# A streaming channel gate: the first 8 rows in a tile of their own, kept on chip and stored last

## Chip, cores, metric

One core of one Trainium2 chip; the rest of the chip is idle. The metric is the device time of one execution in microseconds. Every profile shows the span from the first to the last instruction, which is 1.4 to 1.5 us shorter. One row below is 768 bytes in each of the 128 partitions, 98,304 bytes.

A run is called slow when it lies over 1.5% above the fastest of its kernel; ratios are of fast runs. The experiments were measured in three calls (batches, each with the kernel before in turn), the first two on chip 10 and the third on chip 12; the record doesn't give the chip of the result. PE is the matrix engine, DVE the vector engine, ACT the scalar engine, POOL GpSimd, and SP the engine on whose queue most loads are issued; a transfer lands when the last of the 16 DMA engines has done its share of it.

## The reference, cut to what matters

```python
# x: bf16 [1, 384, 384, 384], w1d: bf16 [1]
g = einsum("bhwc->bc", x) / (H * W)      # mean over all pixels
s = sigmoid(g * w1d[0])                  # k = 1: one weight, no neighbours
return x * s[:, None, None, :]
```

The gate needs the sum over all of x, and of x (113.25 MB) the kernel keeps only a few tiles on the chip at a time. Read strictly, x would have to be read twice.

## The kernel before

It reads x once. It guesses the gate from the mean of the first 4 rows, stores every tile with this guess, sums all of x meanwhile, and compares the true gate with the guess in bf16 at the end. Only if they differ, which this data never makes them do, does it go through x again. x is 1152 rows, 18 tiles of 64 in 4 slots. Of each tile, PE sums 48 rows (matmuls with ones) and DVE 16 rows (`OWN`); DVE also multiplies by the gate. Loads are issued on the SP queue (the second half of tile 0 and all of tile 2 on ACT's), stores on ACT's.

```python
TILE, SLOTS, EARLY, LEAD, FORE, OWN = 64, 4, 4, 8, 32, 16
PAUSE = 9
...
load(0, TILE, 0, hi=LEAD)                             # 8 rows of tile 0, for the guess
plan.dma("sync", w_one[0:1, 0:1], w1d.unsqueeze(0), writes=["w_one"])
load(0, TILE, 0, ("sync", "scalar"), lo=LEAD)         # its other 56, 28 on each queue
load(slot(1), TILE, row0(1))
load(slot(2), TILE, row0(2), ("scalar", "scalar"))
load(slot(3), TILE, row0(3))
...
for k in range(n_tiles):
    if k >= SLOTS:
        for i in range(2) if k == SLOTS else () if k < SLOTS + 2 else (k - SLOTS,):
            sum_own(i)                                # DVE: 16 rows
            put(slot(i), TILE, row0(i), parts=None if i else (FORE, TILE - FORE))
        if k == SLOTS:
            pause(slot(k))       # one ACT activation of 9 rows, once store 0 has landed
        load(slot(k), TILE, row0(k), reads=["pause"] if k == SLOTS else ())
    ...                                               # PE sums the tile
...
put(slot(last), TILE, row0(last), slot(n_tiles))      # last tile: gate, store
sum_own(last)
join_own()                                            # then the check of the guess
```

Of the kernel before, what the change touches and what calls it, by code (L numbers as in the profile page):

```python
# [3 lines left out]
P = 128  # L4
# [5 lines left out]
ACT_F = mybir.ActivationFunctionType  # L10
# [139 lines left out]
def split(n, most):  # L150
    k = -(-n // most)
    return [n // k + (i < n % k) for i in range(k)]
# [3 lines left out]



TILE, SLOTS, EARLY, LEAD, FORE, OWN = 64, 4, 4, 8, 32, 16


PAUSE = 9


def bass_standalone__channel_attn_eca__vision_kernel(
# [5 lines left out]
    B, H, W, C = x.shape  # L171
    assert B == 1 and C == ROW and (B * H * W) % (4 * P) == 0
    n_rows = B * H * W // P
    x_rows, o_rows = x.flatten_outer_dims(), out.flatten_outer_dims()

    def dram(view, r0, n):
        return view[r0 * P : (r0 + n) * P, :].rearrange("(p t) c -> p (t c)", p=P)

    ones = nc.alloc_sbuf_tensor("ones", [P, P], BF16)
    s_early = nc.alloc_sbuf_tensor("s_early", [P, C], BF16)  # L180
    w_one = nc.alloc_sbuf_tensor("w_one", [1, 16], BF16)
    w_scaled = nc.alloc_sbuf_tensor("w_scaled", [P, 2], F32)
    warm = nc.alloc_sbuf_tensor("warm", [P, 2], F32)
# [3 lines left out]
    zeros = nc.alloc_sbuf_tensor("zeros", [P, 2], BF16)  # L187
    own = nc.alloc_sbuf_tensor("own", [P, C], F32)
    part = nc.alloc_sbuf_tensor("part", [P, C], F32)
    terms = nc.alloc_sbuf_tensor("terms", [P, 3 * C], BF16)  # L190
    n_arena = nc.sbuf_bytes_remaining // (2 * C)
    arena = nc.alloc_sbuf_tensor("arena", [P, n_arena * C], BF16)
    acc = [
        [nc.alloc_psum_tensor(f"acc{g}_{i}", [P, WIDE], F32) for i in range(3)]
        for g in range(2)
    ]
# [3 lines left out]
    def at(r0, n):  # L200
        assert r0 + n <= n_arena
        return arena[:, r0 * C : (r0 + n) * C]

    def rows(r0, n):
        return [("sb", r) for r in range(r0, r0 + n)]

    def gate(to, place, n, s):
        s_b = s[:].unsqueeze(1).broadcast_to([P, n, C])
        v, to_v = (at(r, n).rearrange("p (t c) -> p t c", t=n) for r in (place, to))
        return lambda e: e.tensor_tensor(to_v, v, s_b, ALU.mult)  # L210

    n_tiles = n_rows // TILE
    base = SLOTS * TILE
    assert n_rows % TILE == 0 and base + PAUSE <= n_arena
    assert EARLY % 4 == FORE % 4 == (TILE - OWN) % 4 == 0 and EARLY <= LEAD <= FORE
    last = n_tiles - 1
    ready = nc.alloc_semaphore("ready")

    def slot(k):
        return k % SLOTS * TILE  # L220

    def row0(k):
        return k * TILE


    s_true = at(slot(last), 1)
    plan = Planner(nc, "a", 70)

    def load(place, n, r0, queues=("sync",), lo=0, hi=None, reads=()):

        i, hi = lo, hi or n
        for queue, m in zip(queues, split(hi - lo, -(-(hi - lo) // len(queues)))):
            plan.dma(
                queue,
                at(place + i, m),
                dram(x_rows, r0, n)[:, i * C : (i + m) * C],
                reads=reads,
                writes=rows(place + i, m),
            )
            i += m  # L240
# [3 lines left out]
    def mm(e, bank, weights, moving, start, stop):  # L244
        if not loaded:
            loaded.append(e.matmul(bank, weights, moving, start=start, stop=stop))  # L246
            return loaded[0]
        return e.add_instruction(  # L248
            mybir.InstMatmult(
                name=nc.get_next_instruction_name(),  # L250
                engine=mybir.EngineType.PE,
                ins=[e.lower_ap(moving), e.lower_ap(weights)],
                outs=[e.lower_ap(bank)],
                start_tensor_calc=start,
                stop_tensor_calc=stop,
                ldweights=False,
            )
        )

    def add_rows(e, group, column, n, start, stop):  # L260

        n_wide = n * C // WIDE
        all_of = [
            mm(
                e,
                acc[group][i % 3][:, :],
                ones[:],
                arena[:, column + i * WIDE : column + (i + 1) * WIDE],
                start and i < 3,
                stop and i >= n_wide - 3,  # L270
            )
            for i in range(n_wide)
        ]
        return all_of[-1]

    def sum_early():
        plan.op(
            "tensor",
            lambda e: add_rows(e, 0, 0, EARLY, True, True),
            reads=["ones"] + rows(0, EARLY),  # L280
            writes=["acc0"],
        )

    def nothing(e, bank, start):

        none = zeros[:, 0:1].broadcast_to([P, WIDE])
        return mm(e, acc[1][bank][:, :], ones[:], none, start, not start)

    def sum_all():

        def one(e, s):
            e.wait_ge(ready, 1).then_inc(ready, -1)  # L292
            for r, n in ((0, FORE), (FORE, TILE - OWN - FORE)):
                add_rows(e, 1, (slot(s) + r) * C, n, False, False).then_inc(
                    plan.sems["tensor"], 1
                )

        def emit(e):
            for i in range(3):
                nothing(e, i, True)  # L300
            rounds = -(-n_tiles // SLOTS)
            some = n_tiles - (rounds - 1) * SLOTS
            with e.Fori(0, rounds) as k:
                for s in range(some):
                    one(e, s)
                if some < SLOTS:
                    with e.If(k < rounds - 1):
                        for s in range(some, SLOTS):
                            one(e, s)
            for i in range(3):  # L310
                done = nothing(e, i, False)
            done.then_inc(plan.sems["tensor"], 1)

        plan.streams["tensor"].append(("block", emit, None))
# [62 lines left out]
                writes=["acc_own"],  # L377
            )

    def put(place, n, r0, to=None, parts=None):  # L380
        to, i = place if to is None else to, 0
        for m in parts or [n]:
            plan.op(
                "vector",
                gate(to + i, place + i, m, s_early),
                reads=["s_early"] + rows(place + i, m),
                writes=rows(to + i, m),
            )
            i += m
        plan.final.append(  # L390
            plan.dma("scalar", dram(o_rows, r0, n), at(to, n), reads=rows(to, n))
        )

    def pause(r0):

        to = at(base, PAUSE)
        plan.op(
            "scalar",
            lambda e: e.activation(  # L399
                to, warm[:, 0:1].broadcast_to([P, PAUSE * C]), ACT_F.Sigmoid  # L400
            ),
            reads=["warm"],
            writes=rows(r0, 1) + ["pause"],
        )

    def weight():

# [24 lines left out]
    plan.op("gpsimd", lambda e: e.memset(warm[:, 0:1], 0.0), writes=["warm"])  # L432
    plan.op("vector", lambda e: e.memset(ones[:], 1.0), writes=["ones"])  # L433
    plan.op("gpsimd", lambda e: e.memset(zeros[:], 0.0), writes=["zeros"])
    load(0, TILE, 0, hi=LEAD)
    plan.dma("sync", w_one[0:1, 0:1], w1d.unsqueeze(0), writes=["w_one"])
    load(0, TILE, 0, ("sync", "scalar"), lo=LEAD)
    load(slot(1), TILE, row0(1))

    load(slot(2), TILE, row0(2), ("scalar", "scalar"))  # L440
    load(slot(3), TILE, row0(3))
    heads = {e: len(plan.streams[e]) for e in ("sync", "scalar")}
    weight()
    sum_early()
    add_banks(0, copy=True)
    plan.op(
# [4 lines left out]
        reads=["total", "w_scaled0", "warm1"],  # L451
        writes=["s_early"],
    )
    plan.need("tensor", ["zeros"])
    sum_all()

    for k in range(n_tiles):
        if k >= SLOTS:

            for i in range(2) if k == SLOTS else () if k < SLOTS + 2 else (k - SLOTS,):  # L460
                sum_own(i)
                put(slot(i), TILE, row0(i), parts=None if i else (FORE, TILE - FORE))
            if k == SLOTS:
                pause(slot(k))
            load(slot(k), TILE, row0(k), reads=["pause"] if k == SLOTS else ())
        there = rows(slot(k), TILE)
        plan.relay(ready, "gpsimd", "tensor", there, rows(slot(k), FORE), ["acc1"])
        plan.signals("tensor", rows(slot(k) + FORE, TILE - OWN - FORE), ["acc1"])
    plan.signals("tensor", [], ["acc1"])
    for k in range(n_tiles - SLOTS, last):  # L470
        sum_own(k)
        put(slot(k), TILE, row0(k))

    put(slot(last), TILE, row0(last), slot(n_tiles))
    sum_own(last)
    join_own()

# [5 lines left out]
        reads=["acc_own", "total"],  # L483
        writes=["total"],
# [6 lines left out]
        reads=["total", "w_scaled1"],  # L491
        writes=["s_true"] + rows(slot(last), 1),
# [6 lines left out]
        reads=["s_true", "s_early"],  # L499
        writes=["total"],  # L500
# [4 lines left out]
        reads=["total"],  # L505
        writes=["wrong"],
# [4 lines left out]
        reads=["wrong"],  # L511
        writes=["redo"],
# [6 lines left out]
    half, r0 = (base - above) // 2, 0  # L519
    for k, n in enumerate(split(n_rows, half)):  # L520
        place = above + k % 2 * half
# [4 lines left out]
            reads=rows(place, n),  # L526
            writes=rows(place, n),
# [98 lines left out]
```

## Time and profile before

| | before |
|---|---|
| time, 6 runs | 528.34 us median, 527.86 to 529.28 |
| span of the first profile | 526.5 us |
| DVE busy | 440.0 us (84%) |
| PE busy | 180.0 us (34%) |
| DMA | full from 1 to 524 us, 433 GB/s |

The prediction below shows the lines that carry this and reads them.

### The profile page before, as it was taken

What the parts mean: (1) busy time and instruction counts of PE and PEld (TensorE: products, weight loads), DVE (VectorE), ACT (ScalarE), POOL (GpSimd) and SP (SyncE); (2) the same over time, 40 slices, a digit from 0 to 9 for tenths busy, and PEclk for the clock granted to TensorE, in tenths of its full rate; (3) what the DMA queues carried; (4) which work ended last, traced back from release to release, by engine and by line L of the source; (5) the groups of instructions that cost most, each with busy time, mean ns of one, the idle gap of its engine ahead of it and who ended that gap; (6) DMA issues with size and microseconds to landing.
All of it is one profiled execution on the core that took longest, in us unless ns stands there. A gap on an engine that the chain in (4) does not pass through costs nothing.

```text
span 526.5 us, 902 instructions
## 1 busy us (share of the span) xinstructions
PE 180.0 (34%) x648; PEld 0.2 (0%) x2; DVE 440.0 (84%) x78; ACT 5.8 (1%) x5; POOL 0.3 (0%) x6
## 2 busy tenths in 40 slices
PE   2255752043240707061422506070513315070701
PEld 0000000000000000000000000000000000000000
DVE  1869999999996978969696969789696969698795
ACT  1000020000000000000000000000000000000000
POOL 0000000000000000000000000000000000000000
PEclk9996967558585858567575858576675858585765
DMA  9999999999999999999999999999999999999998
GB/s 375 433 459 405 418 448 448 418 418 467 429 418 418 467 429 418 429 459 426 418 429 459 426 418 441 445 429 418 448 437 429 418 459 429 426 418 459 429 426 359
DMA packets 5620, 226.51 MB, mean 430 GB/s; under 512 B 626, under 2 KB 626, under 8 KB 754
## 3 DMA queue, kind: packets, MB, share of 16 engines
q10 hardware_dynamic: 3024, 122.29, 53.7%
q1 hardware_dynamic: 2594, 104.20, 46.0%
q14 instruction: 2, 0.02, 0.0%
HBM read 113.25 MB, written 113.25 MB: 430 GB/s over the span
## 4 chain that ended last, share of the span: by engine, by line
DMA 42%; another core or an unknown queue 27%; DVE 21%; issue 7%; SPq 0%; ACT 0%; DVEq 0%
DMA arena<-in_x_dram 24%; DMA out_dram<-arena 18%; DVE part L338 12%; DVE arena L210 7%; DVE own L345 1%; DVE total L326 0%; SPq L109 0%; DVE own L363 0%; DVE terms L356 0%; ACT arena L488 0%; DVE total L496 0%; DVE total L482 0%; DVE wrong L504 0%; DVE total L324 0%
## 5 line engine op out<-in xcount | busy, mean ns | idle before, releaser
L248 PE MATMUL acc<-arena,ones 128*128 128x512 bf16 x637 | 176.1, 441 | 312.2 <-PEq L292 310.8
L210 DVE TENSOR_TENSOR arena<-arena,s_early 128x24576 bf16<-128x24576 bf16 (+1 forms) x19 | 233.2, 12278 | 11.5 <-PE acc L248 6.5
L338 DVE TENSOR_REDUCE part<-arena 128x384 f32<-128x6144 bf16 x17 | 179.2, 10539 | 56.9 <-DMA arena<-in_x_dram 56.9
L338 DVE TENSOR_REDUCE own<-arena 128x384 f32<-128x6144 bf16 x1 | 10.4, 10435 | 0.6 <-DMA arena<-in_x_dram 0.6
L345 DVE TENSOR_TENSOR own<-own,part 128x384 f32<-128x384 f32 x17 | 9.5, 558 | 0.6
L425 DVE TENSOR_SCALAR w_scaled<-w_all 128x1 f32<-128x1 f32 x2 | 0.2, 152 | 8.0 <-PE w_all L416 8.0
L248 PE MATMUL acc_own<-terms,ones 128*128 128x384 bf16 x3 | 1.4, 479 | 15.3 <-DVE terms L356 15.3
L488 ACT ACTIVATE arena<-total,w_scaled 128x384 bf16<-128x384 f32 x1 | 0.6, 615 | 440.3 <-DVE total L482 440.3
L326 DVE TENSOR_TENSOR total<-total,acc 128x128 f32<-128x128 f32 (+2 forms) x10 | 3.9, 393 | 0.3
L399 ACT ACTIVATE arena<-warm 128x3456 bf16<-128x3456 f32 x1 | 3.1, 3082 | 61.9 <-DMA out_dram<-arena 61.9
L416 PE MATMUL w_all<-w_one,ones 1*128 1x1 bf16 x1 | 0.2, 158 | 9.3 <-DMA w_one<-in_w1d_dram 9.3
L248 PE MATMUL acc<-zeros,ones 128*128 128x512 bf16 x6 | 2.3, 507 | 0.0
L324 DVE COPY total<-acc 128x384 f32<-128x384 f32 x2 | 1.1, 554 | 1.2 <-PE acc L248 1.2
L410 ACT ACT_TABLE_LOAD x1 | 1.3, 1283 | 2.3 <-issue 2.3
L433 DVE MEMSET ones<- 128x128 bf16 x1 | 0.2, 165 | 1.3 <-PEq L611 1.3
L363 DVE TENSOR_TENSOR own<-own,terms 128x384 f32<-128x384 f32 x2 | 1.1, 559 | 0.1
L356 DVE CAST terms<-own 128x384 bf16<-128x384 f32 x3 | 1.1, 359 | 0.1
L496 DVE TENSOR_TENSOR total<-arena,s_early 128x384 f32<-128x384 uint16 x1 | 0.6, 558 | 0.7 <-ACT arena L488 0.7
L448 ACT ACTIVATE s_early<-total,w_scaled 128x384 bf16<-128x384 f32 x1 | 0.6, 614 | 9.8 <-DVE total L326 9.8
L482 DVE TENSOR_TENSOR total<-total,acc_own 128x384 f32<-128x384 f32 x1 | 0.6, 554 | 0.1
L246 PE MATMUL acc<-arena,ones 128*128 128x512 bf16 x1 | 0.6, 608 | 0.0
L504 DVE TENSOR_REDUCE wrong<-total 128x1 f32<-128x384 f32 x1 | 0.6, 553 | 0.0
(10 smaller groups left out, 1.2 us busy)
## 6 DMA issues: line engine op xcount, KB each, us to landing
out_dram<-arena ACTq DMA_DIRECT2D x18, 6144.0 KB, 49.9
arena<-in_x_dram SPq DMA_DIRECT2D x16, 6144.0 KB, 41.8
arena<-in_x_dram ACTq DMA_DIRECT2D x2, 3072.0 KB, 41.5
arena<-in_x_dram ACTq DMA_DIRECT2D x1, 2688.0 KB, 14.0
arena<-in_x_dram SPq DMA_DIRECT2D x1, 2688.0 KB, 21.4
arena<-in_x_dram SPq DMA_DIRECT2D x1, 768.0 KB, 7.8
w_one<-in_w1d_dram SPq DMA_DIRECT2D x1, 0.0 KB
```

What stands on the lines that cost most here:

```text
L210: return lambda e: e.tensor_tensor(to_v, v, s_b, ALU.mult)
L246: loaded.append(e.matmul(bank, weights, moving, start=start, stop=stop))
L248: return e.add_instruction(mybir.InstMatmult(name=nc.get_next_instruction_name(), engine=mybir.EngineType.PE, ins=[e.lower_ap(moving), e.l ...
L324: emit = lambda e, part=part, of=of: e.tensor_copy(part, of)
L326: emit = lambda e, part=part, of=of: e.tensor_tensor(part, part, of, ALU.add)
L338: lambda e: e.reduce_sum(to[:], view, axis=mybir.AxisListType.X),
L345: lambda e: e.tensor_tensor(own[:], own[:], part[:], ALU.add),
L356: lambda e, term=term: e.tensor_copy(term, own[:]),
L363: lambda e, term=term: e.tensor_tensor(own[:], own[:], term, ALU.subtract),
L399: lambda e: e.activation(to, warm[:, 0:1].broadcast_to([P, PAUSE * C]), ACT_F.Sigmoid),
L410: lambda e: e.activation(warm[:, 1:2], warm[:, 0:1], ACT_F.Sigmoid),
L448: lambda e: e.activation(s_early[:], total[:], ACT_F.Sigmoid, scale=w_scaled[:, 0:1]),
```

## The change

The intent: the first 8 rows, from which the gate is guessed, get a place of their own above the four slots and stay there until the end. Their store is the last. Tile 0 shrinks to 56 rows, followed by 17 tiles of 64. The pause used to fill the place above the slots, which is now taken, so it fills `terms`, a small buffer that is used only in `join_own`, in three pieces of 3 rows. PE sums the 8 rows first, in place of three matmuls on zeros, and 8 zeroed pad rows let DVE sum 16 rows of tile 0 as of any other.

```diff
-TILE, SLOTS, EARLY, LEAD, FORE, OWN = 64, 4, 4, 8, 32, 16
-PAUSE = 9
+FIRST, EARLY, HEAD, TILE, SLOTS, FORE, OWN = 8, 4, 56, 64, 4, 32, 16
+PAUSE, PAUSES = 3, 3
...
-        to = at(base, PAUSE)
-        plan.op("scalar", lambda e: e.activation(to, warm[...], ACT_F.Sigmoid), ...)
+        to, of = terms[:, : PAUSE * C], warm[:, 0:1].broadcast_to([P, PAUSE * C])
+        for i in range(PAUSES):
+            plan.op("scalar", lambda e: e.activation(to, of, ACT_F.Sigmoid), ...)
...
-    load(0, TILE, 0, hi=LEAD)
+    plan.op("gpsimd", lambda e: e.memset(at(HEAD, len(pad)), 0.0), writes=pad)
+    load(base, FIRST, 0)
-    load(0, TILE, 0, ("sync", "scalar"), lo=LEAD)
+    load(slot(0), size(0), row0(0), ("sync", "scalar"))
...
-    put(slot(last), TILE, row0(last), slot(n_tiles))
+    gated(base, FIRST)
+    gated(slot(last), TILE, slot(n_tiles))
+    store(slot(n_tiles), TILE, row0(last))
+    store(base, FIRST, 0)
```

More of the change, by code (lines that the diff above doesn't have):

```diff
@@ L210, in gate @@
         return lambda e: e.tensor_tensor(to_v, v, s_b, ALU.mult)
-    n_tiles = n_rows // TILE
+    n_tiles = 1 + (n_rows - FIRST - HEAD) // TILE
     base = SLOTS * TILE
-    assert n_rows % TILE == 0 and base + PAUSE <= n_arena
-    assert EARLY % 4 == FORE % 4 == (TILE - OWN) % 4 == 0 and EARLY <= LEAD <= FORE
+    assert (n_rows - FIRST - HEAD) % TILE == 0 and base + FIRST <= n_arena
+    assert EARLY % 4 == FIRST % 4 == FORE % 4 == (TILE - OWN) % 4 == 0
+    assert EARLY < FIRST and TILE - OWN <= HEAD
     last = n_tiles - 1
@@ L222, in row0, with size, load @@
     def row0(k):
-        return k * TILE
+        return FIRST + (HEAD + (k - 1) * TILE if k else 0)
+    def size(k):
+        return TILE if k else HEAD
     s_true = at(slot(last), 1)
     plan = Planner(nc, "a", 70)
-    def load(place, n, r0, queues=("sync",), lo=0, hi=None, reads=()):
-        i, hi = lo, hi or n
-        for queue, m in zip(queues, split(hi - lo, -(-(hi - lo) // len(queues)))):
+    def load(place, n, r0, queues=("sync",), reads=()):
+        i = 0
+        for queue, m in zip(queues, split(n, -(-n // len(queues)))):
             plan.dma(
@@ L278, in sum_early, with close @@
             "tensor",
-            lambda e: add_rows(e, 0, 0, EARLY, True, True),
-            reads=["ones"] + rows(0, EARLY),
+            lambda e: add_rows(e, 0, base * C, EARLY, True, True),
+            reads=["ones"] + rows(base, EARLY),
             writes=["acc0"],
         )
-    def nothing(e, bank, start):
+    def close(e, bank):
         none = zeros[:, 0:1].broadcast_to([P, WIDE])
-        return mm(e, acc[1][bank][:, :], ones[:], none, start, not start)
+        return mm(e, acc[1][bank][:, :], ones[:], none, False, True)
     def sum_all():
@@ L298, in emit @@
         def emit(e):
-            for i in range(3):
-                nothing(e, i, True)
+            add_rows(e, 1, base * C, FIRST, True, False).then_inc(
+                plan.sems["tensor"], 1
+            )
             rounds = -(-n_tiles // SLOTS)
@@ L310, in emit @@
             for i in range(3):
-                done = nothing(e, i, False)
+                done = close(e, i)
             done.then_inc(plan.sems["tensor"], 1)
@@ L378, in join_own, with gated, store, put @@
             )
-    def put(place, n, r0, to=None, parts=None):
-        to, i = place if to is None else to, 0
-        for m in parts or [n]:
+    def gated(place, n, to=None):
+        to = place if to is None else to
+        plan.op(
+            "vector",
+            gate(to, place, n, s_early),
+            reads=["s_early"] + rows(place, n),
+            writes=rows(to, n),
+        )
+    def store(place, n, r0):
+        plan.final.append(
+            plan.dma("scalar", dram(o_rows, r0, n), at(place, n), reads=rows(place, n))
+        )
+    def put(k):
+        if k:
+            gated(slot(k), TILE)
+        else:
+            gated(slot(k), FORE)
+            gated(slot(k) + FORE, HEAD - FORE)
+        store(slot(k), size(k), row0(k))
+    def pause(r0):
+        to, of = terms[:, : PAUSE * C], warm[:, 0:1].broadcast_to([P, PAUSE * C])
+        for i in range(PAUSES):
             plan.op(
-                "vector",
-                gate(to + i, place + i, m, s_early),
-                reads=["s_early"] + rows(place + i, m),
-                writes=rows(to + i, m),
-            )
-            i += m
-        plan.final.append(
-            plan.dma("scalar", dram(o_rows, r0, n), at(to, n), reads=rows(to, n))
-        )
-    def pause(r0):
-        to = at(base, PAUSE)
-        plan.op(
-            "scalar",
-            lambda e: e.activation(
-                to, warm[:, 0:1].broadcast_to([P, PAUSE * C]), ACT_F.Sigmoid
-            ),
-            reads=["warm"],
-            writes=rows(r0, 1) + ["pause"],
-        )
+                "scalar",
+                lambda e: e.activation(to, of, ACT_F.Sigmoid),
+                reads=["warm"],
+                writes=["pause", "term0", "term1", "term2"] + ([] if i else rows(r0, 1)),
+            )
     def weight():
@@ L434, in bass_standalone__channel_attn_eca__vision_kernel @@
     plan.op("gpsimd", lambda e: e.memset(zeros[:], 0.0), writes=["zeros"])
-    load(0, TILE, 0, hi=LEAD)
+    pad = rows(HEAD, TILE - HEAD)
+    plan.op("gpsimd", lambda e: e.memset(at(HEAD, len(pad)), 0.0), writes=pad)
+    load(base, FIRST, 0)
     plan.dma("sync", w_one[0:1, 0:1], w1d.unsqueeze(0), writes=["w_one"])
-    load(0, TILE, 0, ("sync", "scalar"), lo=LEAD)
+    load(slot(0), size(0), row0(0), ("sync", "scalar"))
     load(slot(1), TILE, row0(1))
@@ L453, in bass_standalone__channel_attn_eca__vision_kernel @@
     )
-    plan.need("tensor", ["zeros"])
+    plan.need("tensor", ["zeros"] + rows(base, FIRST))
     sum_all()
+    plan.signals("tensor", rows(base, FIRST), ["acc1"])
     for k in range(n_tiles):
@@ L461, in bass_standalone__channel_attn_eca__vision_kernel @@
                 sum_own(i)
-                put(slot(i), TILE, row0(i), parts=None if i else (FORE, TILE - FORE))
+                put(i)
             if k == SLOTS:
@@ L465, in bass_standalone__channel_attn_eca__vision_kernel @@
             load(slot(k), TILE, row0(k), reads=["pause"] if k == SLOTS else ())
-        there = rows(slot(k), TILE)
+        there = rows(slot(k), TILE - (0 if k else OWN))
         plan.relay(ready, "gpsimd", "tensor", there, rows(slot(k), FORE), ["acc1"])
@@ L471, in bass_standalone__channel_attn_eca__vision_kernel @@
         sum_own(k)
-        put(slot(k), TILE, row0(k))
-    put(slot(last), TILE, row0(last), slot(n_tiles))
+        put(k)
+    gated(base, FIRST)
+    gated(slot(last), TILE, slot(n_tiles))
+    store(slot(n_tiles), TILE, row0(last))
+    store(base, FIRST, 0)
     sum_own(last)
```

## The prediction

> **What bounds the kernel now.** The kernel reads x once, multiplies each tile by a gate that it guesses from the first 4 rows, stores the product, and sums all of x on the side to check the guess at the end. (A row here is 768 bytes in each of 128 partitions, 98,304 bytes; x has 1152 of them, 18 tiles of 64.) I read the page's head first, to see which engine is full.
>
> ```profile
> span 526.5 us, 902 instructions
> PE 180.0 (34%) x648; PEld 0.2 (0%) x2; DVE 440.0 (84%) x78; ACT 5.8 (1%) x5; POOL 0.3 (0%) x6
> DMA  9999999999999999999999999999999999999998
> HBM read 113.25 MB, written 113.25 MB: 430 GB/s over the span
> ```
>
> No compute engine is full; the DMA row is, in all slices but the last. Bytes read and written are one x each (1152 x 98,304 = 113.25 MB), so there is no traffic to save. A slice of 13 us can hide a gap, so I asked for stretches next. Columns: stretch, length, busy PE, PEld, DVE, ACT, POOL, granted clock, DMA share, GB/s.
>
> ```profile
> 0.00:1.00 1.00, 0.00 (x0) 0.00 (x0) 0.00 (x0) 0.00 (x0) 0.20 (x4) 1.00 0.07 6
> 1.00:524.00 523.00, 179.96 (x648) 0.20 (x2) 440.00 (x78) 5.80 (x5) 0.13 (x2) 0.70 1.00 433
> 524.00:526.00 2.00, 0.00 (x0) 0.00 (x0) 0.00 (x0) 0.00 (x0) 0.00 (x0) 0.50 0.08 29
> ```
> ```profile
> 154.90:183.90 29.00, 10.35 (x35) 0.00 (x0) 24.03 (x4) 0.00 (x0) 0.00 (x0) 0.65 1.00 434
> 183.90:212.90 29.00, 9.51 (x35) 0.00 (x0) 23.98 (x4) 0.00 (x0) 0.00 (x0) 0.71 1.00 434
> ```
>
> The DMA share is 1.00 for 523 us at 433 GB/s, and a period of one tile (one load, one store, 12.58 MB) takes 29.0 us at 434 GB/s whatever the tile. (A packet counts where it starts, so the last 2 us look emptier than they are: packets started before 524 end up to 525.9.) The packet records of the trace say the same: each of the 16 engines runs packets of 49,152 bytes back to back, 1.815 us each, 27.1 GB/s, from 1.0 us until between 524.6 and 525.9 us. Work of another engine counts only if it leaves these engines without a queued transfer. The waits show how far the vector engine is from that:
>
> ```profile
> DVE part L338 <- DMA arena<-in_x_dram: 56.9, 13, 5.3
> DVE arena L210 <- DMA arena<-in_x_dram: 5.0, 1, 5.0
> ```
>
> DVE waits some 5 us for its load in each of the later periods, and not the reverse: it needs 24.0 of the 29.0 us. Last, the end, in the timeline (start, duration, engine, operation):
>
> ```profile
> 471.92 12.95 DVE L210 TENSOR_TENSOR arena<-arena,s_early 128x24576 bf16<-128x24576 bf16 x1
> 484.91 18.34 ACTq L109 DMA_DIRECT2D out_dram<-arena  x2
> 489.92 12.96 DVE L210 TENSOR_TENSOR arena<-arena,s_early 128x24576 bf16<-128x24576 bf16 x1 [5.04 <-DMA arena<-in_x_dram]
> 502.79 10.41 DVE L338 TENSOR_REDUCE part<-arena 128x384 f32<-128x6144 bf16 x1
> ...
> 521.28 0.15 DVE L510 CAST redo<-wrong 128x1 int32<-128x1 f32 x1
> ```
>
> The last load lands at 489.9, the last gate ends at 502.9 and its store is issued then. One 6.29 MB store takes 6.29 / 434 = 14.5 us alone, so it needs the engines from 511.3 to 525.9: when issued it stood 8.4 us behind earlier stores (the completions of the three last stores are at 496.7, 511.3 and 525.9 in the trace). So even here no engine is hungry. The check is done at 521.4, and its readers on the queues are through by about 524.1; that chain has 1.8 us to spare against the last packet. The end is set by bytes, plus 1.0 us before the first packet and 0.5 us after the last.
>
> **What the Trainium skill says.** "DMA: Bandwidth & Descriptors", section "Where 436 GB/s comes from", puts the ceiling at 16 ports x 32 B x 850 MHz = 435.2 GB/s; the trace runs at 433 to 434, within 0.5% of it. The same page, "Queues, rings and completion order", says that each DMA engine takes turns between the queues that have work for it, a packet at a time. This fits: as long as either loads (SP) or stores (ACT) are queued the rate stays at 434, and from 490 on, stores alone run as fast. "VectorE: DVE Perf Modes", section "The perf-mode tier table (the rule you actually need)", has bf16 tensor_tensor at 2x; the gate's 24,576 elements in 12.95 us are 0.527 ns each, two per 0.96 GHz cycle. "Perfetto Trace Analysis", section "Identifying Performance Opportunities", says to improve the most-contended engine; here that is DMA, and the change leaves its bytes alone.
>
> **The change, part by part.**
> 1. *Tile sizes.* 8 + 56 + 17 x 64 = 1152: the same bytes. The opening loads are as before, even in their pieces (8 rows, then 28 on each queue, then tiles 1 to 3); only the 8 rows sit beyond the four slots. They are now contiguous in HBM, but their packets stay 6,144 bytes. The first store is 56 rows, with packets of 43,008 bytes, and there is one more store of 128 packets of 6,144 bytes. At 0.233 us per such packet (median of the first load) and 1.815 x 7/8 = 1.588 for the 56-row ones, an engine's 8 packets of each kind cost 8 x (1.588 + 0.233 - 1.815) = 0.05 us more. On the path: +0.05 us.
> 2. *The gate.* The first tile is gated as 32 + 24 rows instead of 32 + 32, which saves 6.56 x 8/32 = 1.6 us of DVE around 42 us. Its store stands behind a load of tile 2 in the ACT queue, which lands at 53.4, so its issue 1.6 us sooner starts nothing sooner. The 8 rows are gated before the last tile: 3,072 x 0.527 = 1.6 us plus about 0.1. DVE idles 5.0 us there, so it is hidden. On the path: 0.
> 3. *The first store's end, and the pause.* With 8 rows less to move, store 0 lands 8 x 98,304 / 434 GB/s = 1.8 us sooner, near 74 instead of 76. The pause of 3.08 us becomes three: one activation of 3,456 elements at 3.08 and of 1 element at 0.20 give 0.834 ns an element, so 1,152 take 1.16 us, three 3.5, and about 3.6 with two semaphore steps. Load 4 is issued at about 74 + 3.6 = 77.9 instead of 79.2. All that time store 1 (issued at 68.9, 14.5 us of work) is queued. On the path: 0; the phase of loads against stores moves by 1.3 us.
> 4. *The end.* At any time after the first store, 8 more rows have been loaded for the same number stored. So the last load lands 1.3 to 1.8 us sooner, near 488.4; the last gate ends near 501.4; its store starts at about 509.5 behind the older ones, ends at 524.1, and the 8 rows take 1.8 us to 525.9. The check chain ends near 519.8. It had slack already, so this buys nothing.
> 5. *The sum.* Six matmuls on the 8 rows replace three on zeros: about 1.5 us of a PE with 310 us of waits. The GpSimd memset of 8 pad rows is one instruction in the first microseconds, with tile 0 not wanted before 20 us. On the path: 0.
>
> Sum: 527.93 + 0.05 = 528.0 us.
>
> **The rivals.**
> - *The short last store trims the tail.* If the last completion waited on a whole large store, 8 rows would end sooner than 64. For it: a 6.29 MB store is the last thing to land. Against it: each engine moves a fixed share of every store (8 of the 128 packets) and stays busy to its own end, so a smaller last piece leaves each engine's total alone. Its last packet would be 0.23 instead of 1.8 us, and if part of the 1.3 us spread among engines' ends comes from that size, up to 1 us could go: 527.0.
> - *Slack of 8 rows removes a stall.* For it: the tiles' slots are full all the time, and stores gate loads. Against it: the share is 1.00 in every stretch I asked. There is one visible loss, in 44 to 80 us, at 427 instead of 434 GB/s (around 53 us all engines ran one packet of 2.1 to 2.7 us): 36 x 7/434 = 0.6 us. If its cause is the meeting of the first store with loads, it could go or grow: 527.4 to 528.6.
> - *The pause's new phase empties a queue.* Three short activations with waits, an earlier load 4, and a completion of store and load together might leave the engines without work for the 2 us between a landing and the next issue. Against it: in-flight transfers amount to 42 us per load and 50 per store in each 29 us, about three transfers at any time. It would need both queues empty. If it happened in every one of 14 periods, 14 x 1 us: 542; I don't expect it.
> - *The check fails and the second pass runs.* The sum's parts still add to 1152 rows (8 + 48 + 8 for the first 64, with zeros in the pad), so no; it would double the time.
>
> **Range and chances.** The three runs before spread over 0.9 us, and the effects that I can't exclude are each below 1 us either way: 527.2 to 529.1. Two per cent is 10.6 us. Faster by that would need 226.5 MB in about 516 us, 439 GB/s, above anything the trace sustained: 0.01. Slower needs a repeated gap or a second pass: 0.01.
>
> **What would show it right or wrong.** Right: DMA share 1.00 and 433 GB/s from 1 to 524; the last load landing near 488.4 with a DVE gate of about 1.7 us just before it, in a wait that shrinks from 5.0; load 4 issued near 77.9; a store of 8 rows landing at 525.9, about 1.8 us after that of 64 rows; check done near 519.8. Wrong: any stretch after 1 us below 430 GB/s, the last gate waited for by the DMA engines, or engines' last packets ending before 524.5.

## The result, and the profile after

| | before | after |
|---|---|---|
| time, 6 runs | 528.34 us (527.86 to 529.28) | 528.86 us (528.25 to 530.18) |
| ratio, fast runs | | 1.0009, 95% interval 0.9993 to 1.0025: same |
| span of the first profile | 526.5 us | 527.7 us |

A ratio here is the mean time of one kernel's fast runs over that of the other's of the same rounds, so it is not quite the ratio of the medians quoted.

The head of the page of the changed kernel:

```profile
span 527.7 us, 911 instructions
PE 181.6 (34%) x651; PEld 0.2 (0%) x2; DVE 440.1 (83%) x79; ACT 6.2 (1%) x7; POOL 2.9 (1%) x7
DMA  9999999999999999999999999999999999999997
HBM read 113.25 MB, written 113.25 MB: 429 GB/s over the span
```

PE does three matmuls more, DVE one gate more, POOL one memset of 2.7 us, and the bytes are the same. The stretches (columns as in the prediction: length, busy PE, PEld, DVE, ACT, POOL, clock, DMA share, GB/s), first the whole, then two periods of one tile:

```profile
1.00:524.00 523.00, 181.60 (x651) 0.20 (x2) 440.07 (x79) 6.20 (x7) 2.73 (x3) 0.70 1.00 432
524.00:527.40 3.40, 0.00 (x0) 0.00 (x0) 0.00 (x0) 0.00 (x0) 0.00 (x0) 0.50 0.39 161
```
```profile
155.00:184.00 29.00, 10.19 (x35) 0.00 (x0) 23.84 (x4) 0.00 (x0) 0.00 (x0) 0.66 1.00 434
184.00:213.00 29.00, 9.36 (x35) 0.00 (x0) 24.03 (x4) 0.00 (x0) 0.00 (x0) 0.69 1.00 434
```

The bound is untouched: share 1.00, 29.0 us and 434 GB/s for a period. One stretch is slower than the others, before (first line) and after (second):

```profile
44.00:80.00 36.00, 25.32 (x97) 0.00 (x0) 35.55 (x7) 3.08 (x1) 0.00 (x0) 0.79 1.00 427
44.00:80.00 36.00, 25.58 (x99) 0.00 (x0) 35.93 (x6) 3.49 (x3) 0.00 (x0) 0.80 1.02 425
```

Its share is full all the same: packets that take longer count as busy, so only the GB/s show it. DVE's waits for loads are as before too, but for the last (us in total, times, longest):

```profile
DVE part L343 <- DMA arena<-in_x_dram: 58.7, 13, 5.2
...
DVE arena L210 <- DMA arena<-in_x_dram: 3.3, 1, 3.3
```

The pause and load 4, in the timeline, and then the end:

```profile
75.05 3.55 ACT L414 ACTIVATE terms<-warm 128x1152 bf16<-128x1152 f32 x3 [61.37 <-DMA out_dram<-arena]
...
78.63 0.33 SPq L109 DMA_DIRECT2D arena<-in_x_dram  x1
```
```profile
471.60 14.62 DVE L210 TENSOR_TENSOR arena<-arena,s_early 128x24576 bf16<-128x24576 bf16 x2
484.58 18.93 ACTq L109 DMA_DIRECT2D out_dram<-arena  x3
489.55 12.96 DVE L210 TENSOR_TENSOR arena<-arena,s_early 128x24576 bf16<-128x24576 bf16 x1 [3.33 <-DMA arena<-in_x_dram]
...
520.92 0.15 DVE L529 CAST redo<-wrong 128x1 int32<-128x1 f32 x1
```

The first of these lines now holds two gates, the one of tile 16 and that of the 8 rows; 14.62 - 12.95 = 1.7 us is what the new one takes, and DVE's wait for the last load shrank from 5.0 to 3.3 us by as much. The three pauses take 3.55 us.

Two things in the 16 DMA engines' packet records did not look as before. All engines lose some time near 53 us, and one of them, a straggler, ends well after the others:

| profile | loss near 53 us, us per engine | end of the first, median, second-last, last engine |
|---|---|---|
| before | 0.54 | 524.6, 524.9, 525.6, 525.9 |
| after | 1.21 | 524.9, 525.4, 526.0, 527.3 |

The loss is the sum of what load packets of 49,152 bytes took between 40 and 64 us beyond 1.83 us (usual are 1.815), over 16; an engine's end is that of its last store's completion. By these, the 1.2 us between the two profiled spans are one engine's late end (1.3 us after the second-last, against 0.3) and 0.3 to 0.5 us that all engines share.

### The profile page after: what moved, and what is told of

The parts are those of the page before. It is cut to its first block, busy times and chain, and to the rows that moved or that the text cites. A ratio compares the mean times of both kernels' runs of the same rounds, so it can differ in the third digit from the quotient of the medians.

```text
span 527.7 us, 911 instructions
## 1 busy us (share of the span) xinstructions
PE 181.6 (34%) x651; PEld 0.2 (0%) x2; DVE 440.1 (83%) x79; ACT 6.2 (1%) x7; POOL 2.9 (1%) x7
## 4 chain that ended last, share of the span: by engine, by line
DMA 74%; DVE 24%; issue 0%; ACT 0%; SPq 0%; DVEq 0%
DMA arena<-in_x_dram 41%; DMA out_dram<-arena 33%; DVE arena L210 12%; DVE part L343 10%; DVE own L350 1%; DVE total L331 0%; DVE own L368 0%; DVE terms L361 0%; ACT arena L507 0%; DVE total L515 0%; DVE total L501 0%; DVE wrong L523 0%; DVE total L329 0%; SPq L109 0%; DVE redo L529 0%
## 5 line engine op out<-in xcount | busy, mean ns | idle before, releaser
L252 PE MATMUL acc<-arena,ones 128*128 128x512 bf16 x643 | 179.0, 444 | 312.3 <-PEq L296 310.8
L210 DVE TENSOR_TENSOR arena<-arena,s_early 128x24576 bf16<-128x24576 bf16 (+3 forms) x20 | 233.3, 11672 | 9.5 <-PE acc L252 6.2
L414 ACT ACTIVATE terms<-warm 128x1152 bf16<-128x1152 f32 x3 | 3.5, 1162 | 61.4 <-DMA out_dram<-arena 61.4
L449 POOL MEMSET arena<- 128x3072 bf16 x1 | 2.7, 2657 | 0.0
L252 PE MATMUL acc<-zeros,ones 128*128 128x512 bf16 x3 | 0.8, 379 | 0.0
L250 PE MATMUL acc<-arena,ones 128*128 128x512 bf16 x1 | 0.6, 607 | 0.0
```

Source lines behind the costliest of these rows:

```text
L210: return lambda e: e.tensor_tensor(to_v, v, s_b, ALU.mult)
L250: loaded.append(e.matmul(bank, weights, moving, start=start, stop=stop))
L252: return e.add_instruction(mybir.InstMatmult(name=nc.get_next_instruction_name(), engine=mybir.EngineType.PE, ins=[e.lower_ap(moving), e.l ...
L414: lambda e: e.activation(to, of, ACT_F.Sigmoid),
L449: plan.op("gpsimd", lambda e: e.memset(at(HEAD, len(pad)), 0.0), writes=pad)
```

## The experiments

My theory: the time is the bytes at 433 to 434 GB/s, and nothing that was moved lies on that path. The rivals: the short last store changes the tail; the small store or the pause's phase costs by itself; the loss near 53 us makes the difference. Each diff below is against the changed kernel unless it says otherwise, and every ratio is to the kernel before.

### The control, twice

No edit.

> The changed kernel, unaltered, as the control on this chip. Theory (the time is the bytes at 433 to 434 GB/s, and nothing that was moved lies on that path): ratio to the kernel before 1.000 to 1.002. In its profile the loss near 53 us, where every engine's load packet took 2.8 to 3.1 us instead of 1.815 (1.1 us per engine; 0.5 us in the kernel before), should differ from the first profile if it is chance, and so should the one engine that ended 1.3 us after the rest. Rival (the 128 small packets and the late store cost 0.5 to 1 us by themselves): ratio 1.002 or more, and again one engine that ends over 1 us late.

> The changed kernel once more, as the control of this call. Theory: ratio to the kernel before 0.998 to 1.002, and the loss near 50 to 53 us again about 1.1 us per engine, as in all five profiles so far of kernels with the first tile apart.

Measured: 528.42 us median (528.22 to 529.04), ratio 0.9992 (0.9964 to 1.0020), and 528.70 us (528.20 to 530.04), ratio 1.0001 (0.9972 to 1.0030). The loss near 53 us is 1.19 and 1.25 us per engine, so it is not chance; the last engine ends 0.7 and 0.4 us after the second-last instead of 1.3, so that is.

### The kernel before, as a kernel tested

> The kernel before, as one of the kernels tested, to have a second profile of it. Theory: ratio 0.998 to 1.002 to itself. If the loss near 53 us is chance or the chip's, it is anywhere from 0.5 to 1.2 us; if the change doubled it, it is 0.5 us again while the control of this call has 1.1. One engine's end stands out by an amount that differs from profile to profile (0.3 us in its first).

Measured: 528.01 us (527.88 to 528.88), ratio to itself 0.9987 (0.9959 to 1.0016): this is how far one such ratio can be trusted. Loss 0.61 us per engine; ends 524.5, 524.9, 525.7, 526.0. So the change has doubled the loss: 0.54 and 0.61 before, 1.21, 1.19 and 1.25 after (and 1.20 to 1.36 in five more fast profiles of kernels below whose first store is the same 56 rows at the same time).

### No pause

```diff
-PAUSE, PAUSES = 3, 3
+PAUSE, PAUSES = 3, 0
```

> The three pauses taken away; load 4 is then issued as soon as store 0 has landed, at about 75.1 instead of 78.6 us. Theory: same time within 0.2% of the control, since store 1 (14.5 us of work) is queued meanwhile; DMA share 1.00 in 60 to 490 us. Rival (the pause keeps loads and stores in a good phase): 1 us or more slower, with a stretch below 430 GB/s after 75 us.

Measured: 528.89 us (528.09 to 530.25), ratio 1.0001 (0.9972 to 1.0031). In the timeline, load 4 is issued 3.7 us sooner than in the changed kernel:

```profile
74.97 0.33 SPq L109 DMA_DIRECT2D arena<-in_x_dram  x1
```

The last gate starts 2.6 us sooner too (486.92), and the end stays: the time did not come from there. A pause of this length neither costs nor gains anything that these runs resolve.

### A long pause

```diff
-PAUSE, PAUSES = 3, 3
+PAUSE, PAUSES = 3, 15
```

> Fifteen pauses instead of three, 15 x 1.18 = 17.7 us from the landing of store 0 at 75.2. Store 1 is then alone and done at 75.2 + 14.5 = 89.7; load 4 and store 2 (which stands behind the pause on ACT) are issued at 93.0 and start about 1.5 us later. Theory: the 16 engines stand still for 4 to 5 us, which nothing gives back: 533 us, 4.0 to 5.5 above the control. Rival (the vector engine's wait of 5 us in each period is slack in which the pipeline catches up): less than 1 us lost.

Measured: 541.39 us, the median of all five runs; four fast ones from 538.5 to 541.6, ratio 1.0222 (1.0200 to 1.0243), 12 us. The rival that slack makes it up is out, but the size is two to three times what I expected. The profile fell in a slow run (595.8 us), so I read it only up to the gap that the program itself makes, in these stretches:

```profile
60.00:88.00 28.00, 11.94 (x47) 0.00 (x0) 27.97 (x4) 12.78 (x11) 0.00 (x0) 0.79 0.99 429
88.00:94.00 6.00, 0.00 (x0) 0.00 (x0) 6.00 (x2) 4.65 (x4) 0.00 (x0) 0.50 0.43 131
```

Store 1 was done at 88 to 89 us, load 4 and store 2 started at 93.6, 0.8 us after their issue (I had put 1.5): the engines' idle time between 88.0 and 93.7 adds up to 86 engine-us, 5.4 us for each of 16. The other 6 to 7 us of the fast runs have no profile in a fast run, and stay open. Still, one gap of the queues was not given back here: these runs lost at least its length.

### The order of the last two stores, twice

```diff
     gated(base, FIRST)
+    store(base, FIRST, 0)
     gated(slot(last), TILE, slot(n_tiles))
     store(slot(n_tiles), TILE, row0(last))
-    store(base, FIRST, 0)
```

> The 8 rows stored before the last tile instead of after it. Theory: same within 0.2% of the control; the last packets are then 49,152 bytes and the engines' ends spread as in the kernel before (1.3 us). Rival (a short last store trims the tail): 0.5 to 1 us slower than the control.

> The 8 rows stored before the last tile, a second time: the first time its median was 1.5 us above the control's, with runs from 528.5 to 532.1 that overlap it. Theory: chance, so within 1 us of this call's control. Rival (a short last store trims the tail): again 1 us or more above the control.

Measured: 529.93 us (528.48 to 532.05), ratio 1.0027 (0.9995 to 1.0059); the second time 529.12 us (528.01 to 532.30), ratio 1.0009 (0.9975 to 1.0044). The medians are 1.5 and 0.4 us above the controls of their calls, but the lowest runs are not, or hardly (528.48 against 528.22, 528.01 against 528.20). In the profiles the engines end as in the control: first at 524.9, median at 525.4 and 525.3; the last at 526.5 in the first, without any straggler, and at 527.7 in the second, 1.4 us after the second-last. So in the profiles the size of the last store doesn't set where the engines end. The times leave it open: over both calls the twelve runs have a median of 529.37 us and the twelve of the controls 528.54, so 0.8 us, which is in the rival's range although the second pair alone is not. Whether this order makes a late engine more frequent was not tested.

### The 8 rows not stored

Its output is wrong, which doesn't matter for the time.

```diff
     store(slot(n_tiles), TILE, row0(last))
-    store(base, FIRST, 0)
```

> The store of the 8 rows left out (a wrong result, on purpose). Theory: 0.79 MB at 434 GB/s, so 1.8 us less than the control (ratio to it 0.9966), nothing else changed. Rival (another chain, such as the check, which ended 2.1 us ahead of the last packets or so, takes over, or the fixed completion time of a store hides it): less than 1 us gained. Rival (small packets at the end are dearer than their bytes): 2.5 us or more gained.

Measured: 526.89 us (526.38 to 528.73), ratio 0.9960 (0.9932 to 0.9988); over the control's 0.9992 that is 0.9968, 1.7 us, and 1.5 by the medians. Five of the six runs are below every run of both controls. Predicted were 1.8. This is the plainest sign of the bound: 0.7% of the written bytes less, and the time follows by their transfer time. The page confirms what was left out:

```profile
HBM read 113.25 MB, written 112.46 MB: 428 GB/s over the span
```

Its profile is at the same time the best sight of a straggler. 15 engines end between 523.1 and 524.6, 1.7 us before those of the control, and one at 526.9, so this execution took 527.3 us of span, no less than the control's 527.4. One look would have said that the store is free.

### The 8 rows stored first

```diff
+            if k == SLOTS:
+                gated(base, FIRST)
+                store(base, FIRST, 0)
             for i in range(2) if k == SLOTS else ...
...
-    gated(base, FIRST)
     gated(slot(last), TILE, slot(n_tiles))
     store(slot(n_tiles), TILE, row0(last))
-    store(base, FIRST, 0)
```

> The changed kernel with the 8 rows gated and stored first of all, not last: the rows lie apart, but nothing is kept back. Theory: same time within 0.2% of the control; the small store takes its 1.8 us early, so load 4 and the last load come later by about 1.8 us than in the control (last load near 491 instead of 489.4), and the check ends as late as in the kernel before or later, still ahead of the last packets. Rival (what is kept back to the end matters): 1 us or more slower than the control.

Measured: 529.38 us (528.40 to 530.69), ratio 1.0005 (0.9975 to 1.0035). Against the control of its call: 0.7 us in the median, 0.0004 in the ratio, which can't be told from zero. The profiled execution was the slowest of the six (span 529.2): 13 engines ended by 526.0, the others at 526.7, 527.0 and 528.8. (The loss, 0.88 us per engine, came at 58.5 us here, after the first three small packets that each engine moved of the first store.) A straggler does more than end late. Fifteen engines had done their share of the last load by 491.1, the sixteenth at 494.75, and in the timeline the last gate starts right then, at 494.8 instead of 489.2:

```profile
494.77 12.96 DVE L210 TENSOR_TENSOR arena<-arena,s_early 128x24576 bf16<-128x24576 bf16 x1 [4.98 <-DMA arena<-in_x_dram]
```

I had expected 491, which fifteen engines met. As I read it, it still cost only what the last engine was late, because stores were queued meanwhile.

### Tile 2 on the SP queue

```diff
-    load(slot(2), TILE, row0(2), ("scalar", "scalar"))
+    load(slot(2), TILE, row0(2), ("sync", "sync"))
```

> The changed kernel with both loads of tile 2 on the SP queue, so that store 0 stands behind no load and can start when it is issued, at about 42 instead of 51 us. Theory: same time within 0.2% of the control (the bytes are the same, all engines busy either way). If the loss of 1.1 us per engine near 52 us belongs to the meeting of the first store with the loads, it moves to 42 to 47 us; if it belongs to the ACT queue's handing over from loads to stores, it vanishes (0.2% or 1 us faster); if to that time or to tile 3's load, it stays near 50 to 55 us.

Measured: 529.40 us (527.88 to 533.81), ratio 1.0029 (0.9997 to 1.0061); this call has no control of the changed kernel. Tile 0 was ready sooner than I had reckoned, and store 0 went out at 36.3 us. The loss is not near 52 us any more (0.05 us per engine from 42 to 64 us); it is at 37 to 41 us, where load packets of 24,576 bytes took up to 2.2 us instead of 0.91, 1.2 us per engine in all, just ahead of the first store's packets. So it goes with the start of the first store beside loads, and not with tile 3, a fixed time or the ACT queue's change from loads to stores; its size is that of the changed kernel. Nothing was gained, then, and the slower median comes with stragglers: in this profile 13 engines ended at 525.8 to 525.9 and three at 527.2, 527.8 and 529.6. The late ones had made the last load late, and the last store with it, so that the others stood idle for 0.5 us near 509 (7.2 engine-us). The lowest run, 527.88, equals the lowest of the kernel before.

### DVE work beyond the period

```diff
-FIRST, EARLY, HEAD, TILE, SLOTS, FORE, OWN = 8, 4, 56, 64, 4, 32, 16
+FIRST, EARLY, HEAD, TILE, SLOTS, FORE, OWN = 8, 4, 56, 64, 4, 32, 28
```

> The vector engine sums 28 rows of each tile instead of 16: 10.44 x 28/16 = 18.3 us instead of 10.44, so 31.8 us for a tile instead of 24.0, more than the 29.0 that a load and a store take. Theory (DMA binds because DVE has 5.0 us to spare in a period, and no more): DVE becomes the bound; 18 x 7.9 = 142 us more DVE work, of which the 62 us of its waits for loads swallow part: 528.6 + 80 = 608 us, 600 to 614, and no more waits of DVE for loads after the first tiles. Rival (DVE's share of 83% is not real work on the way, and DMA stays the bound): 535 or less.

Measured: 593.90 us (593.79 to 594.17), ratio 1.1244. DVE does become the bound, as these groups and this stretch show (groups: busy us, mean ns, then DVE's idle time before them):

```profile
L343 DVE TENSOR_REDUCE part<-arena 128x384 f32<-128x10752 bf16 x17 | 309.3, 18194 | 0.1
```
```profile
187.00:303.00 116.00, 32.85 (x106) 0.00 (x0) 115.86 (x13) 0.00 (x0) 0.00 (x0) 0.60 0.97 398
```

DVE is busy 115.86 of 116 us, and the 59 us of waits for loads are 0.1. My 608 us was too high. DVE's work grew by 137 us, to 576.8, not by 142. Its idle time up to the check's end fell by 68 us (from 81 in the control to 13), not by 62, since waits for PE went as well; and the check is now what ends last, 2.4 us before the end of the span instead of 6.6. 137 - 68 - 4 = 65 is what was measured (593.9 - 528.6). So DVE's 5 us in each period were real slack in the kernel, and no more than that.

This profile also shows more of the loss. The DMA engines now run out of work at times (none is busy at 138.5 us), and after all 13 places where a load and a store are issued within 4 us of each other, packets take longer again, of loads and of stores: from 139 us loads of 49,152 bytes took up to 3.3 us instead of 1.815, at 173 us stores 2.2 to 2.9, at 175 us loads up to 3.6. After 60 us this adds up to 20.6 us per engine; in the changed kernel it is 0.2. So the loss does not belong to the first store alone. It costs nothing here, where DVE is the bound, and it could be part of the unexplained time of the long pause, which was not tested.

### The first store of the kernel before, in two

```diff
 # against the kernel before; parts is set for tile 0 alone
-        plan.final.append(
-            plan.dma("scalar", dram(o_rows, r0, n), at(to, n), reads=rows(to, n)))
+        for lo, hi in ((0, 56), (56, 64)) if parts else ((0, n),):
+            plan.final.append(plan.dma("scalar", dram(o_rows, r0, n)[:, lo * C : hi * C],
+                              at(to + lo, hi - lo), reads=rows(to + lo, hi - lo)))
```

> The kernel before with its first store cut in two, 56 rows (packets of 43,008 bytes, still 49,152 apart in HBM) and 8 rows. Theory: same time as the kernel before within 0.2%. For the loss near 53 us, 0.5 us per engine in both profiles of the kernel before and 1.1 in all of the changed one's: if the size of the first store's packets sets it, it is 1.1 us here; if the place of the rows or the earlier issue does, 0.5.

Measured: 528.33 us (528.27 to 528.51), ratio 1.0003 (0.9990 to 1.0016). The loss is 0.82 us per engine, between the two kernels' values, so neither answer holds: packets of 43,008 bytes alone don't make it 1.1. Nor is it the issue of the first store: 42.95 us here, and 44.1 and 42.8 in the two profiles of the kernel before.

## Why the prediction was right

The time was predicted as 528.0 us in 527.2 to 529.1; the six runs have a median of 528.86, and the 18 runs of the changed kernel one of 528.61. "Same", at 0.98, holds in every comparison of the two kernels. The middle was too low in part because it started from 527.93, three runs of the kernel before; its six runs have 528.34.

1. *Tile sizes.* Right. The last store's packets took 0.234 us each and those of the 56-row store 1.589, as worked out. That bytes are what counts was shown by leaving the 8 rows out: 1.5 to 1.7 us less, for 1.8 predicted.
2. *The gate.* Right: 1.7 us, taken out of a wait of 5.0 that is now 3.3.
3. *The first store's end, and the pause.* Store 0 landed at 75.0 instead of 76.0, not at 74; the 0.6 us more that all engines lose near 53 us are most of the difference. The pauses took 3.55 us (3.6 predicted), and load 4 went out at 78.63 (77.9 predicted). Without any pause, load 4 went out at 75.0 and the time was the same within the noise, so this step was rightly put at 0 on the path. The rival of an empty queue doesn't come true at 3.55 us; with 17.9 us of pause the engines do stand still, and the time is 12 us longer. The 2 us that this rival puts between a landing and the next issue are in no trace: from load 5 on, each load is issued 0.02 us after the landing that it waits for.
4. *The end.* Mis-sized, with no effect on the time. The last gate was to start at about 488.4 and started at 489.55 (489.29 and 489.15 in the controls; 489.92 and 489.96 before): 0.4 to 0.8 us sooner instead of 1.3 to 1.8. The step that failed is that all 16 engines would come sooner alike. The median engine did its share of the last load at 487.5 instead of 489.0, 1.5 us sooner as predicted, and fifteen were done by 488.3; the sixteenth took until 489.5, and the gate waits for all. The check ended at 521.1, not 519.8, and its slack still covers it. The store of the 8 rows landed 1.8 us after that of the last tile, as predicted, but with a late engine: the last packet ended at 527.3, not 525.9.
5. *PE and POOL.* Right on the path: PE has 310.8 us of waits for its sequencer in both kernels; the memset took 2.66 us at the start and nothing waits for it. One reading was off: tile 0 is wanted not from 20 us but from 13.95, when DVE sums its last 16 rows with the pad; the memset ended at 3.9.

One of the prediction's own signs of being wrong came true: a stretch below 430 GB/s, 425 at 44 to 80 us (417 and 423 in the controls). It was badly chosen, since the same stretch of the kernel before, which the prediction quotes, had 427. It does mark the loss that was named as a rival.

Of the rivals, the trim of the tail by a short last store was not seen: the first and the second-last engine end 1.0 to 1.4 us apart in the changed kernel and 1.0 to 1.1 before, and with the order of the stores exchanged the median engine ends at 525.3 to 525.4, against 525.1 to 525.4. That the exchanged order was 0.8 us slower over both calls stays unexplained. The second rival was the one with something in it: the loss where the first store starts beside loads grew, reproducibly, from 0.54 to 0.61 us per engine to 1.19 to 1.25. That it costs time is not shown. None of the 18 runs of the changed kernel was below 528.20 us, while 18 of 35 runs of the kernel before were, down to 527.84, and the medians are 528.61 and 528.15. But 11 of these 35 were measured on chip 12, where the changed kernel never ran. On chip 10 alone the medians are 528.54 (12 runs) and 528.43 (18), and both means are 528.70. In the profiles the median engine ends at 525.1 to 525.4 in the three of the changed kernel and at 524.9 in the two of the kernel before. So the engines' ends and the lowest runs hint at some tenths of a us, and the times of one chip do not resolve it. No experiment took the loss away; it only moved with the first store. What makes it larger is open: splitting the first store alone gives 0.82.

My sum missed two things: this loss, 0.6 us more per engine, named as a rival but not in the sum, and the engines' unequal ends. I read the ends' spread of 1.3 us as a property of the kernel; it changes from execution to execution, and the last of 16 engines sets the end, up to 2.3 us after the others. That their sum left the median within the range is partly luck: three of the six runs (529.12, 529.13 and 530.18) lie above it. No version that gives the right result was shown to beat the kernel before.

## What to carry to other kernels

When the DMA share is 1.00 over the whole span at a rate that no long stretch exceeds, price a change by its bytes first, and then ask whether it can let the queues run dry: moves of a few microseconds among waits, pauses and gates were free here, a gap of queues was not. A profile of one execution can't resolve differences of a microsecond there, since one late engine out of 16 moved the end by 0 to 2.3 us; look at the median engine's end and at the lowest run as well as at the span, and compare runs of the same chip. To prove that bytes are the bound, leave out a small known transfer and see whether just its time goes.

## What the Trainium skill lacked or had wrong

- "DMA: Bandwidth & Descriptors", "Where 436 GB/s comes from", says that for transfers between HBM and SBUF the HBM side, about 358 GB/s a core, binds. Read alone, that is wrong for these runs: with one core active they sustain 434 GB/s of loads and stores together, close to the 435 that the section gives for the fabric. Elsewhere the skill keeps the 358 to two cores that stream at once.
- The same page's "Rules for kernel authors" ask for 1 MiB or more in each DMA. A store of 0.79 MB queued behind another ran 8 packets an engine at 0.234 us, 1.87 us in all or 420 GB/s, and leaving it out saved 1.5 to 1.7 us: behind other transfers, the smaller size cost a few per cent of itself. The rule leaves this case out.
- No page that I read says how far a core's 16 DMA engines drift apart under full load. Here the last engine ended 0 to 2.3 us after the second-last, and 1 to 4 us after the median, in twelve profiles of this family of kernels.
- Nor does any mention the loss where one queue starts beside the other. At the start of the first store beside loads, load packets of 49,152 bytes took up to 2.7 to 3.4 us instead of 1.815 on all 16 engines (0.5 to 1.4 us each, at 47 to 60 us), and with the first store sooner those of 24,576 bytes up to 2.2 us instead of 0.91 (1.2 us each, at 37 to 41 us). Where DVE was the bound it came back each time a load and a store were issued within 4 us, 20.6 us per engine in all.
